# Attention scores of all eight heads at once, and one written order for the whole first feed-forward layer

## The chip, the core and the metric

The kernel runs on one core of a Trainium2 chip. The time is the device time of one execution in microseconds (us). The kernel before takes 810.61 us (median of 3 runs, 810.53 to 813.6). Its engines are TensorE (PE; its weight loads stand apart as PEld), VectorE (DVE), ScalarE (ACT), GpSimd (POOL) and SyncE (SP), whose queue issues all the kernel's DMAs.

## The reference

Nyström attention over 4 batches, 8 heads, 576 tokens and head size 64, with 32 landmarks (means of 18 tokens each), is followed by two feed-forward layers over the 2304 tokens (512 to 2048 to 512). Inputs come as 64-bit floats.

```python
q_lm = q.reshape(B, H, 32, S // 32, D).mean(axis=3)      # k_lm likewise
A, Bm, C = sm(q, k_lm), sm(q_lm, k_lm), sm(q_lm, k)      # sm: softmax(a @ b.T / 8)
for _ in range(6):
    Z = 2 * Z - Z @ Bm @ Z                               # towards the inverse of Bm
attn = A @ Z @ C @ v
x = attn.transpose(0, 2, 1, 3).reshape(B * S, H * D)
h = x @ w_in;  g = h * clip(h + 3, 0, 6) / 6;  x = g @ w_out      # first layer
h = x @ w_in2; g = where(h > 0, h, exp(min(h, 0)) - 1); out = g @ w_out2
```

## The kernel before

**Slots.** The attention's last product is folded into the first layer's weights, so that the first layer is 128 slots: 4 batches by 2 halves of the tokens by 16 blocks of 128 hidden columns. A half has 288 tokens (320 and 256 in batch 0). In a slot, `slot_a1` makes 6 matmuls of the hidden block (tile h), ACT and DVE apply the activation (gf), ACT and POOL split the result into a rounded part and its rest (gh, gl), and three slots later (`DELAY`) `slot_a2` makes 12 matmuls (tile x): 4 column blocks by the three products of split operands. The 16 slots of batch 0's first half use unsplit operands (g, ub) instead: 4 full-precision matmuls, each of which the profile shows as two instructions. Slots 0 to 15 also convert the first layer's weights from 64 bits.

**Attention of the next batch.** Between the slots of one batch, the next batch's attention is computed ("newton" in the code): `prep` (landmark sums lm on DVE; POOL spreads them into a block-diagonal tile bd with zeros), `score_b` (Bm from lm and bd), `score_c` (C from kt and bd, giving EC), `soft` (A from qt and bd, giving ea), `values` (EC transposed through PE, times v), `inverse` (the iteration, tiles BD, BT and X), `finish`, and `attn_n` (folds the result into the weights w1c, giving nh and nl). Scores are made for one group g of 4 heads at a time: two pairs of heads in each, a matmul with 128 contracted rows and 64 output rows for each pair. All these products go through two PSUM buffers, tile bk; h has two and x four.

**Order.** Up to the end of batch 1 (`second_half`) the order on each engine is written out in PLAN1, one letter for a step ("s" a part of a slot, "c" a step of score_c). From `newton(2)` on, the tile framework's scheduler orders the instructions, by priorities that `wanted` sets and a few dependencies (`gated`, `after`). The second layer's weights are converted there too, one part in every second slot (`conv_out2`, `conv_in2`, `to_dram`): SP loads 64-bit words (tile u), ACT takes two steps, DVE two, POOL one, and the result y is stored when the next part has been loaded (`flush`).

**After slot 127** the second layer begins: `quartet`, `second`, `wino2`.

In the code `act`, `vec`, `pool` and `pe` are thin wrappers that, while `strict[0]` holds, chain each engine's instructions in the order of the code. As nearly every instruction is recorded by such a wrapper, the profile puts nearly all of them on line L116.

Of the kernel before, what the change touches and what calls it, by code (L numbers as in the profile page):

```python
# [31 lines left out]
def nystrom_ffn_kernel(ctx: ExitStack, tc, q, k, v, w_in1, w_out1, w_in2, w_out2, out):  # L32
# [43 lines left out]
    RUN = 6  # L76
# [27 lines left out]
    NAT = 25, 28, 31  # L104

# [265 lines left out]
    PLACES = [f"wo{(kk - 2) % (NKT + 1)}" for kk in range(NKT + 1)]  # L371
# [78 lines left out]
    def load_in2(q):  # L450
# [3 lines left out]
        for kk in range(2):  # L454
# [23 lines left out]
            gated(vec.tensor_tensor(out=f[:, 1], in0=f[:, 0], in1=l[:, 2], op=ALU.add))  # L478
            sub(f[:, 2], f[:, 1], l[:, 0])
            yield  # L480
            gated(sub(f[:, 3], l[:, 1], f[:, 2]))
            sub(f[:, 0], l[:, 0], f[:, 0])
            yield
            gated(act.copy(out=hr[:, 0:3], in_=l[:, 0:3]))
            sub(lr[:, 0:3], l[:, 0:3], h[:, 0:3], pool)
            yield
            gated(act.copy(out=hr[:, 3:7], in_=f))
# [7 lines left out]
    kt_t, qt_t, kbd_t, qbd_t, kl_t = {}, {}, {}, {}, {}  # L495

    def load_qk(b, g, what):
        t = ap_.tile([128, 2, S], F32, name=what + "t", tag=what + "t", bufs=2)
        gated(sp.dma_start(out=t, in_=(k if what == "k" else q)[b, g]))
        raw_t[b, g, what] = t  # L500
# [71 lines left out]
    def score_c(b, g, sc):  # L572
# [23 lines left out]
        if 0 < b < B - 1:  # L596
            load_qk(b + 1, g, "k")
        return EC

    def soft(b, g):  # L600
# [9 lines left out]
        if 0 < b < B - 1:  # L610
            load_qk(b + 1, g, "q")
# [17 lines left out]

    def values(b, g, EC, cvs, sc):  # L630
# [5 lines left out]
        for j in range(RUN):  # L636
            atr(ct[j // JB][0:PRUN, 128 * (j % JB):128 * (j % JB) + 128], EC[:, j:S:RUN], ident)
        yield 1.0
# [112 lines left out]
    def newton(b):  # L751

        EB, sb, sc, cvs = newton_tiles()
        s = [SB * (b - 1) + (NEW if b > 1 else NEW1)]
        kept = {}

        def go(gen, n=99):
            for _ in range(n):
                wanted(s[0])
                try:  # L760
                    s[0] += next(gen) * (PACE if b > 1 else PACE1)
                except StopIteration:
                    return

        def keep(key, gen):
            kept[key] = yield from gen

        go(prep(b, 0))
        go(score_b(b, 0, sb, EB))
        go(keep(0, score_c(b, 0, sc)))  # L770
        go(soft(b, 0))
        go(values(b, 0, kept[0], cvs, sc))
        go(prep(b, 1))
        go(score_b(b, 1, sb, EB))
        inv = keep("Q", inverse(EB, sb))
        sC = keep(1, score_c(b, 1, sc))
        sA = soft(b, 1)
        go(inv, 1)
        go(sC, 2)
        go(inv, 1)  # L780
        go(sC)
        go(inv, 2)
        go(sA, 3)
        go(inv, 2)
        v1 = values(b, 1, kept[1], cvs, sc)
        go(v1, 2)
        go(inv, 2)
        go(sA)
        go(v1)
        go(inv)  # L790
        go(finish(b, kept, cvs, sc))

    PLAN = """  # L800
        wwwwwwwwwmwwlll0123xmykkklmmllklylkwklwbcbkwcblklBcClCacBCwCBwwicivxwwCaiviVaiviaivivaAiyiVAwwxiVyiAwAiaAxiwixViVxAtffwtwyttn
# [123 lines left out]
    def slot_a1(i):  # L925
# [15 lines left out]
        if i < NKT:  # L941
# [13 lines left out]
    def slot_a2(i, mm=smm):  # L955
# [3 lines left out]
        for dm in range(NDM):  # L959
# [3 lines left out]
            if i < NKT:  # L963
                mm(acc[dm], wo[kk][:, sl], gh, kk == 0, kk == NKT - 1)
# [314 lines left out]
    def splits():  # L1279
        for kk in range(NKT):  # L1280
            split_out1(kk)
            yield
# [8 lines left out]
    def first_half(units, n0):  # L1291
# [12 lines left out]
        for i in range(-PRE, NKT):  # L1304
# [25 lines left out]
        for i in range(NKT, END):  # L1330
# [10 lines left out]
    PLAN1 = "sslssssusluulssppllpppssssspspbssosssbsssspssoccbscscpsPacaosvvasvavsosPvPaPasPssossssssssBsPosPssPsPsCCBBsosoCssCsisCsssisiAssAisAsioVssAssVsoiiViVsiiioVsAissisisAsiottifsfssssossnssstnffsTonossnssossnTssnssssnssssssssnTs"  # L1341

    def second_half(slots):

        EB, sb, sc, cvs = newton_tiles()
        kept = {}
# [3 lines left out]

        def parts():
            for c in range(NW):
                yield from attn_n(1, c, 256)

        make = {
            "u": lambda: attn_at(0, 1), "o": splits, "l": lambda: loads(1), "f": lambda: finish(1, kept, cvs, sc), "n": parts,
            "i": lambda: keep("Q", inverse(EB, sb)), "t": lambda: attn_at(1, 0), "T": lambda: attn_at(1, 1),
        }
        for g in range(G):
            for name, gen in (  # L1360
                ("p", lambda g=g: prep(1, g)), ("b", lambda g=g: score_b(1, g, sb, EB)),
                ("c", lambda g=g: keep(g, score_c(1, g, sc))), ("a", lambda g=g: soft(1, g)),
                ("v", lambda g=g: values(1, g, kept[g], cvs, sc)),
            ):
                make[name.upper() if g else name] = gen
        gens = {"s": slots}
        for c in PLAN1.replace(" ", ""):
# [4 lines left out]
        for c in "upbcavPBCAViftnTo":  # L1372
# [171 lines left out]
```

## Time and profile before

| what | value |
|---|---|
| time, median of 3 runs | 810.61 us |
| the profiled execution's own time | 810.39 us |
| its span in the trace | 808.6 us |
| busy share of the span: PE, PEld, DVE, ACT, POOL | 97%, 86%, 67%, 57%, 52% |
| first slot's first matmul, slot 16's, second layer's | at 31.2, 90.2 and 425.7 us |
| PE busy and idle from 90.2 to 425.7 us | 328.5 and 7.0 us |

A matmul's duration in the trace runs from its start to the modelled end of its output, and the next one starts long before that. What a stretch of matmuls costs is therefore read from one start to the next.

### The profile page before, as it was taken

How to read it: one execution, taken by the hardware profiler on the slowest of the kernel's cores; microseconds unless marked ns; L12 is line 12 of the kernel's file. 1: busy time of each engine (PE TensorE's matmuls, PEld its weight loads, DVE VectorE, ACT ScalarE, POOL GpSimd, SP SyncE). 2: the span in 40 equal slices, each digit the busy share in tenths (PEclk: the TensorE clock that was granted, in tenths of full speed). 3: DMA queues.
4: the chain of work that ended last, by engine and by line, in shares of the span. 5: the costliest groups of instructions: out<-in, count | busy, mean ns of one | idle time of the engine just before them, and what ended most of it. 6: DMA issues, size and time to landing. Idle time of an engine off the chain costs nothing.

```text
span 808.6 us, 16376 instructions
## 1 busy us (share of the span) xinstructions
PE 783.2 (97%) x5928; PEld 697.1 (86%) x5928; DVE 541.5 (67%) x1092; ACT 462.0 (57%) x1012; POOL 418.3 (52%) x423
## 2 busy tenths in 40 slices
PE   7799999999999999999999999999999999999998
PEld 6566778789887889889999999888898889999998
DVE  6899677479645764356465777666655655777795
ACT  3687454655556656565555566556544544555562
POOL 2576576467555566464621786769661560223311
PEclk9899999999999999999999999999999999999999
DMA  9977932686667545741542777689998666867663
GB/s 322 404 218 235 304 107 90 206 258 215 205 215 257 162 145 170 235 160 62 184 161 74 260 262 265 236 305 345 387 383 305 225 226 238 278 234 257 226 198 112
DMA packets 115601, 184.58 MB, mean 228 GB/s; under 512 B 8576, under 2 KB 71552, under 8 KB 115520
## 3 DMA queue, kind: packets, MB, share of 16 engines
q1 hardware_dynamic: 115520, 183.54, 66.7%
q8 instruction: 47, 0.77, 0.4%
q14 instruction: 34, 0.28, 0.1%
HBM read 130.02 MB, written 53.48 MB: 227 GB/s over the span
## 4 chain that ended last, share of the span: by engine, by line
PE 71%; DMA 11%; DVE 7%; ACT 3%; issue 3%; POOL 3%; SPq 1%; DVEq 0%; POOLq 0%; ACTq 0%
PE x L116 38%; PE h L116 30%; PE bk L116 4%; DMA u<-in_moe_w_out 3%; DMA qt<-in_q 2%; DVE h L116 1%; DMA kqv<-in_v 1%; DMA un<-in_moe_w_in 1%; DMA ub<-in_moe_w_out 1%; DMA w1d<-w1c 1%; SPq L116 1%; DVE w1c L116 1%; DMA w<-wo2d 1%; DVE lm L116 1%; DVE nl L116 1%
## 5 line engine op out<-in xcount | busy, mean ns | idle before, releaser
L116 PE MATMUL h<-x,wi 128*128 128x384 f32 x1008 | 204.7, 338 | 2.3 <-ACT a L116 1.5
L116 PE MATMUL x<-gh,wo 128*128 128x288 f32 (+1 forms) x896 | 199.3, 297 | 1.5 <-ACT xs L116 1.0
L116 PEld LDWEIGHTS h<-x,wi 128*128 128x128 f32 x1008 | 177.8, 188 | 13.1 <-ACT a L116 2.4
L116 PEld LDWEIGHTS x<-gh,wo 128*128 128x128 f32 x896 | 149.5, 188 | 9.9 <-issue 6.0
L116 PE MATMUL x<-gl,wo 128*128 128x288 f32 (+1 forms) x448 | 131.6, 294 | 0.3 <-DVE gl L116 0.3
L116 ACT CAST gh<-gf 128x288 fp32r<-128x288 f32 (+2 forms) x160 | 72.6, 454 | 88.2 <-DVE gf L116 87.9
L116 POOL TENSOR_TENSOR gl<-gf,gh 128x288 fp32r<-128x288 f32 (+1 forms) x100 | 83.0, 832 | 74.9 <-ACT gh L116 68.8
L116 PE MATMUL x<-w,gh 128*128 128x512 f32 (+1 forms) x360 | 101.8, 356 | 0.1
L116 DVE SCALAR_TENSOR_TENSOR gf<-gf,y 128x384 f32<-128x384 f32 x80 | 65.5, 819 | 33.1 <-ACT gf L116 33.1
L116 PE MATMUL h<-atl,nh 128*128 128x288 f32 (+2 forms) x256 | 81.8, 319 | 4.5 <-DVE nl L116 2.3
L116 PEld LDWEIGHTS x<-gl,wo 128*128 128x128 f32 x448 | 84.3, 188 | 1.6 <-issue 0.9
L116 ACT ACTIVATE gf<-h,half_b 128x288 f32<-128x288 f32 (+2 forms) x128 | 63.7, 498 | 37.3 <-PE h L116 32.0
L116 DVE SCALAR_TENSOR_TENSOR gf<-gf,h 128x288 f32<-128x288 f32 (+1 forms) x112 | 49.5, 443 | 43.7 <-ACT gf L116 42.7
L116 PE MATMUL x<-w,ghl 128*128 128x512 f32 (+1 forms) x324 | 76.7, 356 | 0.2 <-DVE ghl L116 0.2
L116 PE MATMUL h<-ath,nl 128*128 128x288 f32 (+2 forms) x256 | 76.7, 300 | 0.0
L116 ACT ACTIVATE gf<-y 128x384 f32<-128x384 f32 x80 | 42.0, 525 | 60.5 <-DVE y L116 60.4
L116 PE MATMUL h<-ath,nh 128*128 128x288 f32 (+2 forms) x256 | 76.4, 298 | 0.0
L116 PEld LDWEIGHTS x<-w,gh 128*128 128x128 f32 x360 | 64.7, 189 | 6.4 <-ACT gh L116 0.5
L116 PEld LDWEIGHTS h<-atl,nh 128*128 128x128 f32 x256 | 48.6, 190 | 18.5 <-issue 9.0
L116 PE MATMUL x<-w,gl 128*128 128x512 f32 (+1 forms) x180 | 64.2, 357 | 0.0
L116 POOL TENSOR_TENSOR x<-u,gf 128x384 f32<-128x384 f32 x16 | 18.1, 1151 | 85.2 <-DVE gf L116 50.9
L116 PEld LDWEIGHTS x<-w,ghl 128*128 128x128 f32 x324 | 55.2, 189 | 5.9 <-DVE ghl L116 0.4
(182 smaller groups left out, 1526.2 us busy)
## 6 DMA issues: line engine op xcount, KB each, us to landing
wi<-wi2p SPq DMA_DIRECT2D x64, 448.0 KB, 5.8
wi2p<-wi SPq DMA_DIRECT2D x32, 448.0 KB, 2.9
u<-in_moe_w_in SPq DMA_DIRECT2D x25, 512.0 KB, 4.8
w1c<-w1d SPq DMA_DIRECT2D x48, 256.0 KB, 4.3
w<-wo2p SPq DMA_DIRECT2D x24, 512.0 KB, 6.7
ub<-in_moe_w_out SPq DMA_DIRECT2D x16, 512.0 KB, 10.2
u<-in_moe_w_out SPq DMA_DIRECT2D x16, 512.0 KB, 5.3
wo2p<-w SPq DMA_DIRECT2D x16, 512.0 KB, 3.9
```

Source lines behind the costliest of these rows:

```text
L116: inst = getattr(self.eng, name)(*a, **kw)
```

## The change

Six things change.

1. Batches 1 to 3 make their scores for all 8 heads together (`prep8`, `score_b8`, `score_c8`, `soft8`). The helper `products` makes, for a half of the tokens, 8 matmuls with 64 contracted rows and 32 output rows: no block-diagonal tile, no zeros. The key landmarks stand in the key tile's first 32 columns, so that Bm comes out of the same matmuls as C's first half. For this the host hands over the odd group with the two heads of each pair in swapped rows for these batches, and the softmax of C is written back into the key tile. Each call of `products` takes both bk buffers. The part of C that shared a bank with Bm is copied out by ACT first.
2. The order is written out (PLAN1 anew, PLAN2, PLAN3, `ending`) for the whole first layer; `newton` and the scheduler's freedom there are gone.
3. The second layer's weights are converted by `conv_stream`, two parts loaded ahead; a converted part is stored ahead of the next load instead of behind it. Steps "z" of the plans place it.
4. Slots 14 and 15 use split operands (`FULL = 14`), so that their 8 full-precision instructions each become 12 split ones, and their weights are split in steps "h".
5. The start's plan (PLAN) has another order, with 30 warming matmuls instead of 25, and slots 1 and 2 have 3 and 4 instead of 7 and 2.
6. Some dependencies (`gated`) of the second layer's first weights go.

```diff
+    FULL = 14
-        if i < NKT:
+        if i < FULL:
             g = gp.tile([128, T2], F32, name="g", tag="gh")[:, 0:nt]
...
+    def products(ps, w, x, gs):
+        for pr in range(2):
+            for a in range(2):
+                o = 64 * pr + 32 * a
+                for i, g in reversed(list(enumerate(gs))):
+                    r = slice(64 * (a ^ g), 64 * (a ^ g) + 64)
+                    amm(ps[i][o:o + 32, :], w[i][r, pr, :], x[i][r, pr, :], True, True)
...
+    def score_c8(b, gs, sc, first):
+        kt, ql = [kt_t[b, g] for g in gs], [ql_t.pop((b, g)) for g in gs]
+        EC = [t[:, 0, 32:] for t in kt]
+        cut = 0, 32 + HALF, 32 + S
+        for hf in range(2):
+            ps.append([bank()[:, 0:cut[hf + 1] - cut[hf]] for _ in gs])
+            products(ps[hf], ql, [t[:, :, cut[hf]:cut[hf + 1]] for t in kt], gs)
+            yield 0.4
+            if hf == 0 and b:
+                for i in n:
+                    act.copy(out=EC[i][:, 0:HALF], in_=ps[0][i][:, 32:])
...
+    def soft8(b, gs):
+        for hf in range(2):
+            sa.append([bank()[:, 0:HALF] for _ in gs])
+            products(sa[hf], [t[:, :, 0:32] for t in kt], [t[:, :, hf * HALF:(hf + 1) * HALF] for t in qt], gs)
...
+    def conv_stream():
+        def begin():
+            o, src, k = conv.pop(0)
+            u = room()
+            y = stg.tile([128, W], F32, name="y", tag="y", bufs=YB)
+            gen = steps(src, u, y.rearrange("p (k n) -> p k n", k=k) if k > 1 else y)
+            next(gen)
+            return gen, o, y
+        nxt = [begin(), begin()]
+        while nxt[0]:
+            gen, o, y = nxt.pop(0)
+            flush()
+            nxt.append(begin())
+            yield
+            for _ in gen:
+                yield
+            pending.append((o, y))
...
-                for _ in range((2, 7, 2)[i]):
+                for _ in range((2, 3, 4)[i]):
...
-    second_half(first_half(units, n0))
-    strict[0] = False
-    newton(2)
+    batch(1, PLAN1, first_half(units, n0), zs, (256,))
+    for b, plan in ((2, PLAN2), (3, PLAN3)):
+        batch(b, plan, slots_of(SB * b - SB + 4, SB * b + 4), zs)
+    ending(slots_of(NA - SB + 4, NA), zs, load_x(0, vec), load_in2(0))
+    strict[0] = False
```

How this moves instructions is shown at three places. On PE, the first score products of batch 3 stood so before (lm with bd is Bm's product, kt with bd a half of C's for one group; h and x are slots):

```order
L116 MATMUL bk<-lm,bd 64x32 x2
L116 MATMUL x<-gh,wo_1966 128x288
L116 MATMUL x<-gl,wo_1966 128x288
L116 MATMUL bk<-kt,bd 64x288 x2
L116 MATMUL x<-gh,wo_1966 128x288 x2
L116 MATMUL x<-gl,wo_1966 128x288
L116 MATMUL x<-gh,wo_1966 128x288
```

Now the products of both groups, Bm's among them, stand in one block of 8 matmuls:

```order
L117 MATMUL x<-gh,wo_1451 128x288
L117 MATMUL bk<-kt,lm 32x320 x8
L117 MATMUL x<-gh,wo_1451 128x288
L117 MATMUL x<-gl,wo_1451 128x288
L117 MATMUL x<-gh,wo_1451 128x288 x2
```

Such a batch had 16 matmuls of 64 by 288 and 4 of 64 by 32; it now has 8 of 32 by 320 and 24 of 32 by 288, in four blocks. The second place is PE at the start of the inverse of batch 2 (BD and BT fill one bk buffer each, and DVE reads both). Before:

```order
L116 MATMUL bk<-BD,onesbd 128x128
L116 MATMUL x<-gh,wo_1873 128x288
L116 MATMUL x<-gl,wo_1873 128x288
L116 MATMUL bk<-BT 32x32 x8
L116 MATMUL x<-gh,wo_1873 128x288
L116 MATMUL h<-atl,nh_1884 128x288
L116 MATMUL h<-ath,nl_1885 128x288
L116 MATMUL h<-ath,nh_1884 128x288
```

Now:

```order
L117 MATMUL bk<-BD,onesbd 128x128
L117 MATMUL bk<-BT 32x32 x8
L117 MATMUL x<-gh,wo_1648 128x288
L117 MATMUL x<-gl,wo_1648 128x288
L117 MATMUL x<-gh,wo_1648 128x288
L117 MATMUL bk<-qt,kt 32x288 x8
```

Before, 34 slot matmuls stood between BT and the next bk product; now 3 do, and the product behind them wants both bk buffers. The third place is SP's queue where the second layer's weights begin to be converted (u is a load, wo2d the store of a converted part, w1c folded weights). Before:

```order
L116 DMA u<-in_moe_w_out 128x1024
L116 DMA w1c<-w1d 128x4x128 x4
L116 DMA wo2d<-y 128x512
L116 DMA u<-in_moe_w_out 128x1024
L116 DMA wo2d<-y 128x512
L116 DMA w_5896<-wo2d 128x512
```

Now:

```order
L117 DMA w1c<-w1d 128x4x128 x4
L117 DMA u<-in_moe_w_out 128x1024 x3
L117 DMA w1c<-w1d 128x4x128 x4
L117 DMA wo2d<-y 128x512
L117 DMA u<-in_moe_w_out 128x1024
L117 DMA w_5915<-wo2d 128x512
L117 DMA wo2d<-y 128x512
```

Three loads now stand ahead of the first store; behind it stores and loads alternate. PE's order in the second layer is the same as before.

## Rows read from the trace of the kernel before

**Rows 1.** Stretches: length, busy PE, PEld, DVE, ACT, POOL; clock, DMA share, GB/s.

```profile
0.00:31.20 31.20, 22.65 (x345) 17.01 (x345) 22.80 (x72) 12.58 (x32) 10.42 (x31) 0.98 0.96 351
31.20:90.20 59.00, 55.22 (x367) 39.57 (x367) 52.20 (x96) 45.62 (x93) 40.34 (x32) 0.95 0.82 266
90.20:425.70 335.50, 328.46 (x3096) 290.72 (x3096) 206.20 (x458) 194.44 (x456) 185.85 (x205) 1.00 0.56 181
425.70:808.60 382.90, 376.91 (x2125) 349.85 (x2124) 260.30 (x468) 209.37 (x433) 181.70 (x155) 1.00 0.73 254
```

**Rows 2.** Groups of PE instructions, 90.2 to 425.7 us: the three score products.

```profile
L116 PE MATMUL bk<-qt,bd 128*64 128x288 f32 x48 | 8.3, 429 | 0.6 <-ACT EC L116 0.4 <-DVE nn L116 0.2
L116 PE MATMUL bk<-kt,bd 128*64 128x288 f32 x48 | 8.0, 426 | 0.1
L116 PE MATMUL bk<-lm,bd 128*64 128x32 f32 x24 | 2.1, 233 | 0.7 <-POOL bd L116 0.7
```

**Rows 3.** PE in order of time (start, us, instruction) around score blocks of batch 3.

```profile
254.15 0.29 PE L116 MATMUL x<-gl,wo 128*128 128x288 f32 x1
254.38 0.71 PE L116 MATMUL bk<-kt,bd 128*64 128x288 f32 x4
255.01 0.53 PE L116 MATMUL x<-gh,wo 128*128 128x288 f32 x2
...
272.39 0.31 PE L116 MATMUL bk<-lm,bd 128*64 128x32 f32 x4
272.62 0.40 PE L116 MATMUL h<-atl,nh 128*128 128x288 f32 x1
...
277.58 1.19 PE L116 MATMUL bk<-kt,bd 128*64 128x288 f32 x8
278.70 0.40 PE L116 MATMUL h<-atl,nh 128*128 128x288 f32 x1
278.94 0.29 PE L116 MATMUL h<-ath,nl 128*128 128x288 f32 x1
279.07 0.29 PE L116 MATMUL h<-ath,nh 128*128 128x288 f32 x1
```

**Rows 4.** PE in order of time around two blocks of 64 by 32 matmuls (attn_n).

```profile
151.29 0.66 PE L116 MATMUL bk<-w1c,mt 64*32 64x256 f32 x16
151.89 0.40 PE L116 MATMUL h<-atl,nh 128*128 128x288 f32 x1
...
333.09 1.09 PE L116 MATMUL bk<-w1c,mt 64*32 64x512 f32 x16
334.11 0.40 PE L116 MATMUL h<-atl,nh 128*128 128x288 f32 x1
```

**Rows 5.** PE in order of time around slot 12's full-precision matmuls.

```profile
87.91 0.31 PE L116 MATMUL h<-ath,nh 128*128 128x320 f32 x1
88.06 2.32 PE L116 MATMUL x<-g,ub 128*128 128x320 f32 x8
90.17 0.36 PE L116 MATMUL h<-atl,nh 128*128 128x256 f32 x1
```

**Rows 6.** Two of PE's waits, 90.2 to 425.7 us: in total, times, longest.

```profile
PE bk L116 <- DVE nl L116: 2.4, 3, 1.2
PE bk L116 <- POOL bd L116: 0.7, 2, 0.4
```

**Rows 7.** PE: a block of 64 by 32 matmuls that found a bk buffer taken.

```profile
146.81 0.99 PE L116 MATMUL bk<-w1c,mt 64*32 64x256 f32 x16 [0.42 <-DVE nl L116]
```

**Rows 8.** PE's BD in batch 0, and DVE's steps that read BD's and BT's buffers.

```profile
14.75 0.46 PE L116 MATMUL bk<-BD,onesbd 128*128 128x128 f32 x2 [0.72 <-DVE BT L116]
...
15.25 0.29 DVE L116 TENSOR_REDUCE nn<-bk 128x4 f32<-128x128 f32 x1 [0.43 <-PE bk L116]
...
16.25 0.41 DVE L116 SCALAR_TENSOR_TENSOR X<-bk,cc,istack 128x32 f32<-128x32 f32 x2
```

**Rows 9.** ACT's exponentials over a half of C (durations min, median, max).

```profile
L116 ACT ACTIVATE EC<-bk,mx x16: 484/493/501, 12.7 to 282.3; 128x288 f32<-128x288 f32 x16
```

**Rows 10.** DMA issues on SP, KB each, median us to landing.

```profile
ub<-in_moe_w_out SPq DMA_DIRECT2D x16, 512.0 KB, 10.2
u<-in_moe_w_out SPq DMA_DIRECT2D x16, 512.0 KB, 5.3
```

More of the change, by code (lines that the diff above doesn't have):

```diff
@@ L595, in score_c @@
             )
-        if 0 < b < B - 1:
-            load_qk(b + 1, g, "k")
         return EC
@@ L628, in soft, with prep8 @@
         e_t[b, g] = ea
+    def prep8(b, g):
+        x = kt_t[b, g] = raw_t.pop((b, g, "k"))
+        y = qt_t[b, g] = raw_t.pop((b, g, "q"))
+        lm = ql_t[b, g] = ap_.tile([128, 2, 32], F32, name="lm", tag="lmk", bufs=2)
+        for o, i in ((x[:, :, 0:32], x[:, :, 32:]), (lm, y)):
+            for r in (slice(0, 1), slice(1, 2)):
+                gated(vec.tensor_reduce(
+                    out=o[:, r], in_=i[:, r].rearrange("p r (l c) -> p r l c", c=POOL), axis=AX, op=ALU.add
+                ))
+                yield 0.7
@@ L749, in newton_tiles @@
         return EB, sb, sc, cvs
[L751 to L791, printed above, removed]
     PLAN = """
-        wwwwwwwwwmwwlll0123xmykkklmmllklylkwklwbcbkwcblklBcClCacBCwCBwwicivxwwCaiviVaiviaivivaAiyiVAwwxiVyiAwAiaAxiwixViVxAtffwtwyttn
+        wwlwkwwwl0w1wlmk2lww3lymxwykmlkmlykwkbwkbwkccbwlwyBClCalyclcBlCwCBwiwcxwvwiawvCiviawiaViviivaAiyiVAwxyxiViAwAiaAiwxixiVxVwAtfxwftywttwn
     """
@@ L1277, in nystrom_ffn_kernel, with splits @@
     NA = B * SB
-    def splits():
-        for kk in range(NKT):
+    def splits(kks):
+        for kk in kks:
             split_out1(kk)
@@ L1329, in first_half, with slots_of @@
         run(ns)
-        for i in range(NKT, END):
+        yield from slots_of(NKT, END)
+    def slots_of(n0, n1):
+        for i in range(n0, n1):
             wanted(i)
@@ L1345, in second_half, with batch, preps @@
+    def batch(b, plan, slots, zs, narrow=()):
         EB, sb, sc, cvs = newton_tiles()
-        kept = {}
+        kept, first, gs = {}, [], range(G)
         def keep(key, gen):
             kept[key] = yield from gen
+        def preps():
+            for g in gs:
+                yield from prep8(b, g)
         def parts():
             for c in range(NW):
-                yield from attn_n(1, c, 256)
+                yield from attn_n(b, c, *narrow)
         make = {
-            "u": lambda: attn_at(0, 1), "o": splits, "l": lambda: loads(1), "f": lambda: finish(1, kept, cvs, sc), "n": parts,
-            "i": lambda: keep("Q", inverse(EB, sb)), "t": lambda: attn_at(1, 0), "T": lambda: attn_at(1, 1),
-        }
@@ L1359, in second_half @@
[L1359 to L1367, printed above, removed]
+            "p": preps, "c": lambda: keep("C", score_c8(b, gs, sc, first)), "b": lambda: score_b8(gs, first, sb, EB),
@@ L1368, in second_half @@
+            "i": lambda: keep("Q", inverse(EB, sb)), "a": lambda: soft8(b, gs),
+            "v": lambda: values(b, 0, kept["C"][0], cvs, sc), "V": lambda: values(b, 1, kept["C"][1], cvs, sc),
+            "f": lambda: finish(b, kept, cvs, sc), "n": parts, "t": lambda: attn_at(b, 0), "T": lambda: attn_at(b, 1),
+        }
+        gens = {"s": slots, "z": zs, "u": attn_at(0, 1), "o": splits(range(FULL)), "l": loads(1), "h": splits(range(FULL, NKT))}
+        for c in plan:
             if c not in gens:
@@ L1371, in second_half, with ending @@
         run(slots)
-        for c in "upbcavPBCAViftnTo":
+        for c in "pcbiavVftnT":
             run(gens[c] if c in gens else make[c]())
-        for e in (act, vec, pool):
-            e.flow = e.last
+        if b == 1:
+            run(gens["o"])
+    def ending(slots, zs, xs, ws):
+        for i in range(NA - SB + 4, NA):
+            for n in range(NDM + 1):
+                next(slots, None)
+                if i < NA - SB + XSET + 4:
+                    next(zs, None)
+                elif n == 2:
+                    next(xs, None)
+                if i >= NA - 22 and n == 4:
+                    next(ws, None)
+        run(slots)
+        run(zs)
+        run(xs)
+        run(ws)
     win, xp = [], []
```

169 lines of the change are left out of this document (108 added, 61 removed).

## The prediction

> **What bounds the kernel now.** I read the stretches first [rows 1]. In the second layer, from 425.7 us on, PE is idle 382.9 - 376.9 = 6.0 us in 382.9. In the stretch that the change rebuilds, slots 16 to 127 with the attention of batches 1 to 3 between them (90.2 to 425.7 us), it is idle 335.5 - 328.5 = 7.0 us, while DVE, ACT and POOL are busy 61%, 58% and 55% of it, at full clock. So PE bounds both, and a matmul taken out of the stretch shortens it, as long as no wait takes its place. The 31.2 us before the first slot are a chain of loads and small steps (PE busy 22.7), and the 59 us of slots 0 to 15 are shared by PE (55.2) and DVE (52.2).
>
> Next I read what the scores cost PE. The groups count 48 + 48 + 24 instructions in the stretch [rows 2], but their durations overlap, so the price is read in order of time, from start to start [rows 3]. The usual step between slot matmuls is 0.13 us (278.94 to 279.07). A block of 4 instructions of 288 columns takes 255.01 - 254.38 = 0.63, one of 8 takes 278.70 - 277.58 = 1.12, one of 4 with 32 columns 272.62 - 272.39 = 0.23. Ahead of a block the step is 0.23 instead of 0.13 (254.15 to 254.38), and behind it 0.24 (278.70 to 278.94): every block costs another 0.2 us at its two ends.
>
> **The change part by part.**
>
> *Scores.* Batches 1 to 3 have 6 blocks of the small kind, 16 of four and 4 of eight (16 x 4 + 4 x 8 = 96, the two groups of 48; 6 x 4 = 24). That is 6 x 0.23 + 16 x 0.63 + 4 x 1.12 = 15.9 us, with 26 x 0.2 = 5.2 for the ends 21.1 us. The new blocks have 16 instructions each, of 64 by 32. The trace has this form in attn_n [rows 4]: 16 instructions of 256 columns take 151.89 - 151.29 = 0.60, of 512 columns 334.11 - 333.09 = 1.02, so 0.00164 a column: 0.65 at 288 and 0.70 at 320 columns. These blocks too go through the column groups in the outer loop and through the two row halves, each with its own bank, in the inner one, just as `products` does. Three batches have 3 x 0.70 + 9 x 0.65 = 8.0 us, and 12 x 0.2 = 2.4 for the ends: 10.4. The difference is -10.7 us. With bd gone, PE's waits for it go too, -0.7 [rows 6]. From below: if blocks with both row halves ran no better than one half at a time, the 0.00164 a column would double and the 12 blocks would cost 12 x 0.48 = 5.8 more, leaving -5.6. I take -11.4, since the form is measured in this very kernel.
>
> *Slots 14 and 15.* 8 full-precision instructions take 90.17 - 88.06 = 2.11 us; 12 split ones at the 320-column step of 0.15 (87.91 to 88.06) take 1.8 [rows 5]. Two slots: -0.6. The weights' split comes earlier and the rounded copies and rests of two slots are new, about 1 us each on ACT and POOL beside PE; the price is 0 if they are ready in time and some 1 us if x of slot 14 waits for them.
>
> *Two banks at a time.* Here the change adds waits. A score block for both groups needs both bk buffers, and PE runs in order, so that a block that finds one taken stops the slots behind it. The trace shows this wait: such a block of attn_n waits 0.42 us with its instruction stream spread out [rows 7], and these waits come to 2.4 us [rows 6]. The nearest place in the new order is behind BD and BT. From BD's start to the end of DVE's last read of BT's buffer it is 16.25 + 0.41 - 14.75 = 1.9 us [rows 8]. BD and BT with the three slot matmuls that now follow take about 0.7 + 0.4 = 1.1, so qt,kt waits some 0.8 us, in batch 2 and again in batch 3; in batch 1 the first X is as near: together 2.4. In batch 1 the two key blocks stand 18 slot matmuls of 256 columns (2.2 us) apart, while emptying the first takes a maximum, an exponential and a copy for each group, some 3 us, and behind the second four exponentials of 0.5 with their sums [rows 9]: up to 1 each, 2.0. Against these 4.4, of the 7.0 us of idle time that PE has there now, 6.3 without bd's, I expect half to go, since their places are written anew: -3.2. Net +1.2, with -4 (all present waits gone and half the new ones) and +8 (the bank waits nearly twice as long, all present waits still there) as its ends.
>
> *The Trainium skill on this.* "TensorEngine Tiling (Array Packing)", Restrictions and Gotchas, PSUM Pressure, says that row tiling raises the pressure on PSUM, because row tiles that run together write different banks. The trace agrees, with the 0.42 us above. By that rule alone the bank waits would be the price of the faster products; here that is the 4.4 us already in the sum, and the second rival if they grow.
>
> *Written order, conversions.* The number of conversion steps is unchanged, 32 parts of five instructions. In PLAN2 95 "z" steps at five a part make 19 parts in the 101 us of 32 slots, 5.3 us a part, and the load stands two parts ahead, over 10 us before ACT wants it. The loads land in 5.3 us [rows 10], so they are hidden; ACT's 6 new copies of half a C (some 3 us) lie beside PE, as ACT is idle 42% of the stretch. The earlier store only frees y sooner. Price 0; if the lead fails, the third rival.
>
> *Start.* The order of the start has changed, and there are 5 more warming matmuls early and 4 - 2 = 2 fewer in slots 1 and 2 on balance. The loads of q, k, v are as before. No row shows the new order; its bounds are -2 and +2 us (PE is idle 31.2 - 22.7 = 8.5 us there, and a quarter of it either way is what a reordering of the small steps may move). I take 0. The second layer's PE order is the same, so I take 0 there, with 1 us either way for when its first operands are ready.
>
> Sum: -11.4 - 0.6 + 1.2 = -10.8 us against the profiled execution's own 810.4 us, of which 808.6 is its span: 799.6. That execution lies 0.2 below the median of the runs, so I say 799.8.
>
> **The rivals.**
> *Everything in the order gets better too.* The new plans may remove most of the 7.0 us of idle time in the stretch, and some of the step ends, with hardly a new wait, and the start gains its 2 us: -11.4 - 0.6 - 4 - 2 = -18, 792.4. For it: letters that were moved one by one can fit what each step waits for. Against it: the new bank waits, which no order with two bk buffers avoids altogether.
> *Bank waits take it back.* The four score blocks, BD, BT and the transposes all take bk buffers in turn. At +8 for them the sum is -11.4 - 0.6 + 8 = -4, 806.4. For it: the 0.42 us wait and the 3 slot matmuls behind BT. Against it: in batches 2 and 3 the key blocks have 33 to 48 slot matmuls (4.4 to 6.4 us) behind each for DVE and ACT, but for the pair in batch 3 with 24.
> *Row halves don't run together.* Then -5.6 takes the place of -10.7: 804.9. Against it stand the two rows of attn_n.
> *Slower: loads hold ACT.* With every engine in a written order, an ACT step whose load hasn't landed stops the next slots' activations, and with two h buffers PE stops two slots later. It decides from the point where a load takes longer than its lead of about 10 us; ub, the same size, took 10.2 in the first stretch [rows 10], at a DMA share of 0.82 to 0.96 [rows 1] against 0.56 here. At 0.7 us for each of 32 loads it is +22 - 10.8, 821.8. For it: nothing in the stretch now, with its 5.3 us.
>
> **How the numbers follow.** The forecast, from 796 to 803, has a chance of 0.58; the better order 0.16; the bank waits 0.14; the halves 0.04; slower 0.08. What a measurement of this kernel can tell from no change is about 0.5%, 4 us: faster means below 806.6. The forecast, the better order, the halves and about 0.05 of the bank waits lie there, 0.83; the rest of the bank waits and 0.01 of the slower case lie within 0.5%, 0.10; slower is 0.07. A range of 792 to 806 leaves out the slower case, some of the bank waits and the tail of the better order.
>
> **What would show it.** In the profile after: the blocks of kt with lm and of qt with kt should take 0.65 to 0.70 us from start to start (1.13 if the halves don't overlap). Slot 16 should begin within 2 us of 90.2 and the second layer's first matmul at about 415 instead of 425.7, with the rest as long as now, 382.9. PE's waits for DVE's X and nn at bk should be near 1 us each in place of bd's. If ACT's waits for u are long and h waits for gf, the slower rival holds. The prediction is wrong if the stretch from 90.2 us shortens by less than 5 or more than 16 us, or if the gain lies elsewhere.

## The result and the profile after

The changed kernel takes 805.26 us (median of 11 runs, 803.13 to 808.08); the kernel before, on the same chip, 812.92 us. The ratio is 0.9918, with a 95% interval of [0.9895, 0.9941]; two more sets gave 0.9908 and 0.9917. So it is faster, by about 6.6 us of 810.6, where 10.8 were forecast. 805.26 us lies inside the range of 792 to 806, but outside the forecast's own 796 to 803; by the ratio it is 804.0 on the scale of 810.6 us, which lies between the same bounds.

The page of the profiled run (804.58 us, span 802.5), busy time by engine and the granted clock in 40 slices:

```profile
PE 777.6 (97%) x6014; PEld 697.7 (87%) x6014; DVE 537.7 (67%) x1092; ACT 465.2 (58%) x1020; POOL 411.7 (51%) x401
PEclk9799999999999999999999999999999999999999
```

Its stretches, as [rows 1] shows those of before (slot 16 begins at 89.9 us, the second layer at 417.75):

```profile
31.00:89.90 58.90, 55.18 (x360) 39.31 (x360) 52.21 (x96) 45.03 (x93) 41.25 (x33) 0.91 0.85 274
89.90:253.00 163.10, 159.49 (x1746) 139.19 (x1745) 101.23 (x245) 102.68 (x246) 96.96 (x99) 1.00 0.67 210
253.00:275.00 22.00, 18.06 (x143) 16.52 (x142) 19.00 (x46) 11.99 (x29) 12.90 (x12) 0.92 0.84 248
275.00:417.75 142.75, 142.17 (x1293) 133.58 (x1291) 79.89 (x170) 82.42 (x188) 69.10 (x71) 1.00 0.43 144
417.75:802.50 384.75, 377.54 (x2126) 349.73 (x2124) 261.81 (x469) 209.01 (x433) 181.03 (x155) 1.00 0.73 253
```

The rebuilt stretch has become 335.5 - 327.85 = 7.65 us shorter, where the sum had 10.8, and the second layer 1.8 longer. In the stretch nearly half of PE's idle time, 3.9 of 8.1 us, lies in 22 us around 260, where the granted clock is also low. The views of PE's waits from 89.9 to 417.7 us, to set beside [rows 6]:

```profile
PE h L117 <- DVE gf L117: 4.3, 2, 3.9
PE bk L117 <- ACT kt L117: 1.3, 2, 0.8
PE bk L117 <- DVE lm L117: 1.2, 1, 1.2
PE bk L117 <- DMA vt<-in_v: 0.6, 1, 0.6
PE bk L117 <- DVE nn L117: 0.4, 1, 0.4
```

Of before's waits only the one for nn is left, and a new one, for gf, is the longest. The score blocks themselves, in PE's order of time (start, duration, instructions, wait):

```profile
109.12 0.71 PE L117 MATMUL bk<-qt,kt 64*32 64x288 f32 x16
109.77 0.39 PE L117 MATMUL x<-gh,wo 128*128 128x256 f32 x1
...
176.23 0.49 PE L117 MATMUL bk<-BD,onesbd 128*128 128x128 f32 x2
177.22 0.33 PE L117 MATMUL bk<-BT 32*32 32x32 f32 x16 [0.51 <-ACT kt L117]
...
178.07 1.23 PE L117 MATMUL bk<-qt,kt 64*32 64x288 f32 x16
179.24 0.41 PE L117 MATMUL x<-gh,wo 128*128 128x288 f32 x1
...
277.60 1.53 PE L117 MATMUL bk<-qt,kt 64*32 64x288 f32 x16
279.06 0.40 PE L117 MATMUL x<-gh,wo 128*128 128x288 f32 x1
```

From start to start a free block takes 109.77 - 109.12 = 0.65 us, as forecast. Behind BD and BT of batch 2 it takes 1.17, the extra 0.52 inside the block; BT had already waited 0.51 for the other buffer. In batch 3 the same block takes 279.06 - 277.60 = 1.46, 0.81 more than a free one. The profile counts most of such a wait inside a block as PE's busy time, so the list above leaves it out. Of the twelve blocks six take 0.64 to 0.71 us, one 0.79 and five 0.95 to 2.66: 12.1 us in all with the waits inside them, where the sum had 8.0 without any.

The stop at 256 us, first PE, then ACT, DVE, GpSimd and SyncE in the same view:

```profile
255.57 0.29 PE L117 MATMUL x<-gh,wo 128*128 128x288 f32 x1
259.80 0.40 PE L117 MATMUL h<-atl,nh 128*128 128x288 f32 x1 [3.94 <-DVE gf L117]
...
261.18 0.44 PE L117 MATMUL x<-gh,wo 128*128 128x288 f32 x1
261.42 0.44 PE L117 MATMUL x<-gl,wo 128*128 128x288 f32 x1
...
253.10 0.43 ACT L117 CAST ath<-at 128x288 fp32r<-128x288 f32 x1
258.20 0.66 ACT L117 ACTIVATE y<-u 128x512 f32<-128x512 f32 x1 [4.67 <-POOL y L117]
258.77 0.48 ACT L117 ACTIVATE gf<-h,half_b 128x288 f32<-128x288 f32 x1
...
255.54 1.17 DVE L117 SCALAR_TENSOR_TENSOR y<-u,y 128x512 uint32<-128x512 uint32 x1
256.64 1.40 DVE L117 TENSOR_REDUCE kt<-kt 128x32 f32<-128x576 f32 x2
257.96 1.40 DVE L117 TENSOR_REDUCE lm<-qt 128x32 f32<-128x576 f32 x2
259.29 0.46 DVE L117 SCALAR_TENSOR_TENSOR gf<-gf,h 128x288 f32<-128x288 f32 x1
...
253.91 1.32 POOL L117 TENSOR_TENSOR y<-y,u 128x512 uint32<-128x512 uint32 x1 [1.68 <-issue]
...
255.25 0.33 SPq L117 DMA_DIRECT2D wi2d<-y  x1
```

This is the seam of two written plans. PLAN2 ends in `TzznzzzzzTz` and PLAN3 begins `ppzps`: nine conversion steps (z) and three landmark steps (p) stand between two slot steps (s); T and n are other attention steps. ACT can't begin the next part (y<-u, 258.20) before one of the two y buffers is free: GpSimd's sum of the part two before ends at 255.23, its store is issued at 255.25, and the stores here land in 2.1 to 2.9 us, up to 258.15. (The view names the next sum, which ends at 258.13, so this profile alone doesn't tell the two apart. In the two other profiles of the changed kernel it names the store, with 5.1 and 4.7 us.) The slot's gf on ACT stands behind that, at 258.77. On DVE two conversion steps and four landmark sums (2.8 us; the fourth is recorded two slot steps behind the seam) stand ahead of its gf, which comes at 259.29. Both queues would have held PE. ACT's wait in the second profile:

```profile
ACT y L117 <- DMA wi2d<-y: 5.1, 1, 5.1
```

Behind the stop the steps are 0.24 us (261.18 to 261.42) and not 0.13, in 16 matmuls, 16 x 0.11 = 1.8 us. In the stretches there the clock is the third figure from the end, and PE is idle 3.8 of 4 us ahead of its fall:

```profile
256.00:260.00 4.00, 0.20 (x1) 0.20 (x2) 4.00 (x7) 1.80 (x4) 1.44 (x2) 1.00 1.02 323
260.00:263.50 3.50, 3.50 (x16) 3.50 (x16) 2.57 (x6) 1.44 (x4) 1.65 (x2) 0.52 1.01 294
263.50:267.00 3.50, 3.50 (x37) 2.82 (x36) 2.63 (x9) 2.82 (x7) 2.41 (x3) 1.00 0.59 149
```

0.52 is the level of 1.2 GHz for nearly all of the 3.5 us. Stop and clock together cost 3.9 + 1.8 = 5.7 us.

The wait for lm comes from a load of u. ACT, DVE and PE where the conversions begin, in batch 2:

```profile
162.33 0.66 ACT L117 ACTIVATE y<-u 128x512 f32<-128x512 f32 x1 [2.56 <-DMA u<-in_moe_w_out]
...
163.02 0.43 DVE L117 TENSOR_SCALAR y<-y 128x512 uint32<-128x512 uint32 x1 [1.79 <-ACT y L117]
...
164.68 0.75 DVE L117 TENSOR_REDUCE lm<-qt 128x32 f32<-128x576 f32 x1
...
165.48 0.74 PE L117 MATMUL bk<-kt,lm 64*32 64x320 f32 x8 [1.25 <-DVE lm L117]
```

The first load of u is issued at 156.02, behind four loads of w1c. ACT waits for it from 159.77, DVE's conversion step waits for ACT, and the last landmark sum stands behind that step in DVE's order. In the three profiles of the changed kernel ACT waits 2.56, 3.06 and 1.95 us for this load, and PE 1.25, 1.75 and 0.66 us for lm, 1.3 less each time.

### The profile page after: what moved, and what is told of

It reads as the page before. It is cut to its first block, busy times and chain, and to the rows that moved or that the text cites. A ratio compares the mean times of both kernels' runs of the same rounds, so it can differ in the third digit from the quotient of the medians.

```text
span 802.5 us, 16527 instructions
## 1 busy us (share of the span) xinstructions
PE 777.6 (97%) x6014; PEld 697.7 (87%) x6014; DVE 537.7 (67%) x1092; ACT 465.2 (58%) x1020; POOL 411.7 (51%) x401
## 4 chain that ended last, share of the span: by engine, by line
PE 61%; DVE 3%; DMA 2%; POOL 1%; ACT 1%; issue 1%; DVEq 0%; ACTq 0%; POOLq 0%
PE x L117 33%; PE h L117 27%; PE bk L117 2%; DMA wi<-wi2d 1%; POOL x L117 1%; DMA x<-wo2d 1%; DVE u L117 0%; DVE y L117 0%; DVE gf L117 0%; DVE ghl L117 0%; DVE gl L117 0%; ACT gf L117 0%; ACT ghl L117 0%; DVE kt L117 0%; DVE lm L117 0%
## 5 line engine op out<-in xcount | busy, mean ns | idle before, releaser
L117 PE MATMUL x<-gh,wo 128*128 128x288 f32 (+2 forms) x912 | 207.2, 299 | 0.0
L117 PEld LDWEIGHTS x<-gh,wo 128*128 128x128 f32 x912 | 154.4, 189 | 14.0 <-issue 12.3
L117 PE MATMUL x<-gl,wo 128*128 128x288 f32 (+2 forms) x456 | 133.8, 293 | 0.0
L117 POOL TENSOR_TENSOR gl<-gf,gh 128x288 fp32r<-128x288 f32 (+2 forms) x102 | 84.8, 831 | 88.4 <-ACT gh L117 75.9
L117 ACT CAST gh<-gf 128x288 fp32r<-128x288 f32 (+3 forms) x162 | 73.7, 455 | 93.9 <-DVE gf L117 92.8
L117 DVE SCALAR_TENSOR_TENSOR gf<-gf,h 128x288 f32<-128x288 f32 (+2 forms) x114 | 50.6, 444 | 68.7 <-ACT gf L117 68.4
L117 DVE SCALAR_TENSOR_TENSOR gf<-gf,y 128x384 f32<-128x384 f32 x80 | 67.9, 849 | 34.3 <-ACT gf L117 34.2
L117 PEld LDWEIGHTS x<-gl,wo 128*128 128x128 f32 x456 | 86.3, 189 | 0.0
L117 POOL TENSOR_TENSOR x<-u,gf 128x384 f32<-128x384 f32 x16 | 18.1, 1151 | 85.1 <-DVE gf L117 50.9
## 6 DMA issues: line engine op xcount, KB each, us to landing
ub<-in_moe_w_out SPq DMA_DIRECT2D x16, 512.0 KB, 10.2
```

The lines of the kernel that those rows point to most:

```text
L117: inst = getattr(self.eng, name)(*a, **kw)
```

## The experiments

The table reads every profile by slots: a slot begins at the first of its 6 matmuls of h, so the starts are counted off PE's timeline. Times in us.

| kernel | slots 16-36 | 36-64 | 64-76 | 76-96 | second layer | ratio to before, 95% |
|---|---|---|---|---|---|---|
| before | 70.2 | 89.1 | 37.1 | 61.2 | 383.0 | 1 |
| after | 64.6 | 85.6 | 40.2 | 59.3 | 384.8 | 0.9918 [0.9895, 0.9941] |
| after, again | 65.2 | 87.5 | 40.6 | 59.3 | 383.6 | 0.9908 [0.9882, 0.9935] |
| after, third | 65.3 | 85.1 | 40.2 | 59.3 | 383.3 | 0.9917 [0.9893, 0.9941] |
| landmarks spread | 64.6 | 85.0 | 40.5 | 59.3 | 384.4 | 0.9903 [0.9873, 0.9933] |
| conversions spread | 67.2 | 86.9 | 39.6 | 59.3 | 383.0 | 0.9912 [0.9883, 0.9941] |
| both | 65.3 | 85.1 | 38.9 | 59.3 | 383.2 | 0.9884 [0.9854, 0.9915] |
| both, again | 65.5 | 84.3 | 39.2 | 59.3 | 383.9 | 0.9902 [0.9864, 0.9939] |
| both, w1c earlier | 65.1 | 87.4 | 38.1 | 59.3 | 384.0 | 0.9886 [0.9859, 0.9913] |
| thin seam | 64.9 | 86.6 | 36.0 | 69.1 | 382.7 | 0.9988 [0.9966, 1.001] |
| thin seam, steps put back | 65.2 | 87.2 | 40.8 | 68.5 | 383.2 | 1.0011 [0.9987, 1.0035] |
| thin seam, stores by GpSimd | 67.1 | 95.3 | 36.1 | 78.0 | 384.0 | 1.0172 [1.0141, 1.0203] |
| thin seam, w1c earlier | 67.1 | 87.1 | 36.0 | 63.5 | 384.2 | 0.9932 [0.9904, 0.9959] |
| store behind load | 66.0 | 90.3 | 42.7 | 61.1 | 382.6 | 1.001 [0.9989, 1.0032] |
| halves one by one | 65.7 | 85.7 | 40.2 | 59.3 | 383.3 | 0.9901 [0.987, 0.9933] |
| slots 14, 15 unsplit | 68.4 | 85.9 | 41.0 | 59.3 | 383.3 | 0.9913 [0.9886, 0.9939] |
| after, conversions late | 65.4 | 82.9 | 35.8 | 59.3 | not read | none |
| before, conversions late | 71.3 | 86.7 | 36.3 | 59.7 | not read | none |

How far one profile can be trusted shows in slots 16 to 36, whose order is the same in all kernels but the two of before and the one with slots 14 and 15 unsplit (with the halves one by one it differs inside the score blocks alone). They take 64.6 to 66.0 us in twelve profiles and 67.1 or 67.2 in three, in which the granted clock from 89 to 157 us was 0.97 instead of 1.00. Slots 36 to 64 differ by 2.4 us between the three profiles of the changed kernel.

**The seam.** The changed kernel again, and the two moves apart and together (each pair of lines is an excerpt of a plan; the blanks in it are there for reading alone):

> The changed kernel once more, on the same chip as the next three. Both theories: the stop of PE at 255.6 us (3.9 us, ended by DVE's gf) and the half clock behind it (0.76 granted between 260 and 267 us) stand at the same place, since every engine's order is fixed; the time is about 0.992 of before. The second layer's extra 1.8 us hangs on when one load lands (wi from wi2d, 5.6 us against 3.9 before): if that is chance, it is not the same in this profile; if the order causes it, it is.

```diff
 landmarks spread (PLAN3's start)
-ppzpsspzszzss sppssss sssss szzpspzcbcsszzs
+zspszpszzspsp sspspss spsspss szzszcbcsszzs
```

> Only the eight landmark steps at the start of batch 3's plan are spread, one or two between slot steps, instead of four in a row ahead of slot 68's second half; the conversions stay. Theory A (the written order holds PE at the seam of the two plans: on DVE four landmark sums, 2.8 us, on ACT a conversion that waits for its y buffer, stand ahead of gf): ACT's own gf still comes at 258.8, so at most 0.5 us is gained here, some -0.2 +- 1 us against the changed kernel. Theory B (DVE's queue alone sets the stop): 2 to 2.8 us less, and less of the half clock: -3 to -4 us.

```diff
 conversions spread (PLAN2's end, PLAN3's start)
-ssszss sssszzs ssszszs zszssss TzznzzzzzTz
+szsszss szssszzs ssszszs zszsszss TznzT
-sppssss sssss
+sppsszss szsszss
```

> Only six of the eight conversion steps at the end of batch 2's plan are moved, three to the slots ahead and three to the slots behind; the landmark steps stay in a row. Theory A: ACT's gf is free early, DVE loses three or four conversion steps of 0.4 to 1.2 us ahead of the landmark sums; the stop shrinks from 3.9 to 1 or 2 us: -2 to -3 us against the changed kernel. Theory B (DVE's queue alone): the same DVE steps go, -2 to -2.5. Theory C (the conversions' rate is what is short, so that moved steps wait elsewhere): within 1 us of the changed kernel, with new waits of PE for gf at other slots.

> Both moves. Theory A: the stop at the seam goes with the half clock behind it, 3.9 + 1.7 = 5.6 us less than the changed kernel, some -5 with a small wait left; about 799 to 800 us beside 810.4 for before, ratio 0.986. Theory B: as theory A, but most of it already in the run with the landmark steps alone. Theory C: -1 us at best, and the missing microseconds come up as waits for gf, lm or kt elsewhere in batches 2 and 3.

The stop stood at the same place again, 4.4 us long. The landmarks alone gained nothing in slots 64 to 76, as theory A had it and B not; the conversions alone some 0.8 us, less than expected, and nothing in the ratio. Both together brought 1.2 to 1.4 us there, each against the mean of the changed kernel's three profiles, and 2.4 to 3.0 in the sum of slots 36 to 96, not 5. PE's rows in that kernel show why:

```profile
256.50 0.40 PE L117 MATMUL h<-atl,nh 128*128 128x288 f32 x1 [1.14 <-DVE gf L117]
...
262.12 0.74 PE L117 MATMUL bk<-kt,lm 64*32 64x320 f32 x8 [0.79 <-DVE lm L117]
...
267.12 0.98 PE L117 MATMUL bk<-kt,lm 64*32 64x288 f32 x16 [0.89 <-ACT EB L117]
```

The long stop is now three short ones and one of 0.26 us, with the full clock (1.00) behind each, and the steps of DVE and ACT are as many as before. The pair of both moves and the changed kernel was run once more:

> The kernel with both moves once more, beside the changed kernel on one chip. Theory A (the stop and its half clock cost the changed kernel 5.6 us, of which a smaller wait for gf, lm and EB takes 3 back): 2 to 3 us less than the changed kernel. Rival (chance): within 1 us of it.

> The changed kernel beside the other three on one chip: ratio 0.991 to 0.992, the stop at the seam at the same place in the trace.

0.9902 against 0.9917, 804.5 against 805.3 us: the same sign, inside the intervals. A gain of 1 to 2 us is likely and not shown.

**Thinner still.** Eight conversion steps out of PLAN2's end and ten out of PLAN3's start (the last 32 of PLAN3 find nothing left to convert, so nothing is lost), batch 3's landmark steps spread, and batch 2's a few steps earlier (those aren't in the excerpt):

```diff
-zszssss TzznzzzzzTz  ppzpsspzszzss sppssss sssss szzpspzcbcsszzs
+zszssss TnT          spsspsps      spsspsps spspsss sscbcsss
```

> Around the seam of the plans of batches 2 and 3 the conversion steps are taken out (9 in batch 2's plan, 10 in batch 3's; the last 32 conversion steps of batch 3's plan did nothing so far, and now do), the landmark steps of batch 3 are spread, those of batch 2 moved a few steps ahead. Theory A (too many steps of other engines between two slot steps at the seam): no wait for gf, lm or EB is left between 250 and 270 us, no half clock there, and the wait for lm at 164 us shrinks: 5 to 7 us less than the changed kernel, 799 to 800 us beside 812 for before, ratio 0.984 +- 0.002. Theory C (the conversions' rate is short): the conversions that are now later collide with batch 3's scores, new waits for gf between 270 and 330 us, ratio 0.988 or more, no better than with both moves.

The seam did as expected: 36.0 us for slots 64 to 76, 4.2 to 4.6 less. The time did not: 6 to 7 us worse than the changed kernel. SyncE's queue and then PE, in order of time:

```profile
319.77 0.33 SPq L117 DMA_DIRECT2D u<-in_moe_w_in  x1
329.06 0.32 SPq L117 DMA_DIRECT2D wi2d<-y  x1
329.48 0.37 SPq L117 DMA_DIRECT2D u<-in_moe_w_in  x1
329.94 2.05 SPq L117 DMA_DIRECT2D w1c<-w1d  x4
...
337.09 1.96 PE L117 MATMUL bk<-w1c,mt 64*32 64x512 f32 x16 [7.06 <-DMA w1c<-w1d]
```

The store at 329.06 waits 9 us in the queue for GpSimd's sum, and the load of w1c stands behind it. Three kernels test this: the steps put back away from w1c, the stores issued by GpSimd, and w1c's load recorded one step earlier.

> As the kernel with the conversion steps taken out around the seam, but these steps are put back where they don't reach the loads of w1c: three more in the last slots of batch 2's plan, seventeen spread over slots 73 to 85, so that the conversions end at about the same slot as in the changed kernel. Theory D (two things decide: nothing but slot steps and landmark sums at the seam, and no store that waits for its data ahead of a w1c load in SP's queue): slots 64 to 76 stay at 36 us instead of 40.2, the wait of 7.1 us for w1c is gone, slots 76 to 96 at 59 to 61 us; 799 to 801 us, ratio 0.985 to 0.987. Theory C (the conversions' rate is short between slots 68 and 96): what the seam gains, slots 76 to 85 lose in waits for gf, ratio 0.991 or more.

> The kernel with the conversion steps taken out around the seam, and nothing else changed but that GpSimd's queue issues the stores of converted parts instead of SyncE's. Theory D (in that kernel PE's 7.1 us for w1c came of a store that waited for its sum in SP's queue, 319.8 to 329.1 us, with the load of w1c behind it): the w1c loads go out when PE frees their buffer, the wait is 0 to 1 us, the half clock behind it is gone, -7 to -9 us against that kernel, ratio 0.988 to 0.990, if issuing costs GpSimd little; each issue of a us there would lengthen gl and bring waits for gl instead. Rival (the load itself is late or slow, whatever stands ahead of it in the queue): the wait for w1c stays at 5 us or more, ratio 0.997.

```diff
 w1c earlier (attn_n, batches 2 and 3)
+            if b > 1 and o + n == W and nb < B:
+                load_w1(nb, nc_)
             yield
-        nb, nc_ = ...
-        if 0 < nb < B:
+        if b <= 1 and 0 < nb < B:
             load_w1(nb, nc_)
```

> The kernel with the conversion steps taken out around the seam, and the loads of w1c for batches 2 and 3 recorded one step of attn_n earlier, so that in SP's queue they stand ahead of up to three stores of converted parts; PE's order is the same. Theory D (the queue's order made the 7.1 us): no wait for w1c and no half clock behind it, slots 76 to 96 at 59 to 60 us instead of 69.1, slots 36 to 96 at 181 to 183; 798 to 801 us, ratio 0.984 to 0.987. Theory C (the number of conversions is the price): the wait moves to gf or to y, slots 36 to 96 stay at 187 us or more, ratio 0.991 or more.

> The kernel with both moves at the seam, with the same earlier loads of w1c. In it PE never waits for w1c, so theory D expects the time of the kernel with both moves within 1.5 us (ratio 0.986 to 0.990); if its remaining 1.3 us wait for gf at 255 us came of SP's queue (a store 1.8 us late behind eight w1c loads), up to 2 us less.

With w1c's load earlier, and PE's order the same, the wait for w1c is gone and slots 76 to 96 take 63.5 instead of 69.1 us: the queue's order had made it. The rest moved to gf (2.7 us at 343.5, and 0.79 granted behind it), so 0.9932 is still no better than the changed kernel. Theory D is half right. Putting the steps back between slots 73 and 85 took the seam's gain away (40.8 us again, with waits for bank buffers that ACT held) and PE stopped for 4.1 us for gf at 325 us, as theory C had it. With the stores on GpSimd's queue the wait for w1c stayed, 8.2 us: in SyncE's queue the loads of u, which wait for the same sum to free their buffer, now held it (three loads issued from 333.1 to 347.5, w1c's at 347.6). Here the Trainium skill has a rule: "DMA: Bandwidth & Descriptors", Issuing engines are not separate DMA queues, says that transfers of all issuers run on the same 16 engines and that another issuer saves only its time to issue. Nothing in the run speaks against it: from GpSimd's queue the stores landed in 4.6 us, no sooner than from SyncE's (2.3 and 3.1 in the changed kernel). On which engines they ran, and why they took longer, it doesn't show. That kernel lost another 8.7 us in slots 36 to 64 (95.3 against 86.6); each store took GpSimd some 0.9 us, but that this is the cause isn't shown.

**The order of store and load,** put back as it was before:

```diff
-            flush()
             nxt.append(begin())
+            flush()
```

> Only the converted part's store goes behind the next load again, as before the change. Theory A (the return of the y buffer stands on the chain that ends ACT's wait at the seam: add, store, landing, next step): each store comes later by the load ahead of it, 0.4 us of issue and what the load waits for, its u buffer; the stop at 255.6 us grows by 0.5 to 3 us, and ACT waits for y at other slots too: +1 to +4 us against the changed kernel. Rival (the forecast's price of 0, the store only has to come some time): the same time within 1 us.

It costs some 8 us: 7.5 to 8.3 by the ratios, 8.3 in slots 36 to 96 (194.0 against 185.7 in the mean). ACT's waits from 156 to 346 us in that kernel, and its stores' time to landing:

```profile
ACT y L117 <- DMA wi2d<-y: 15.0, 10, 3.8
ACT y L117 <- DMA wo2d<-y: 10.3, 7, 2.2
```
```profile
wo2d<-y SPq DMA_DIRECT2D x16, 256.0 KB, 4.5
wi2d<-y SPq DMA_DIRECT2D x16, 256.0 KB, 4.5
```

Behind a load of 512 KB a store lands in 4.5 us instead of 2.3 and 3.1, and ACT waits 25 us for y, where the changed kernel has 7.1 (4.7 at the seam and 2.4 for stores elsewhere). It was more than expected, and it came by theory A's way; how much of it is the later issue and how much the slower landing, the run doesn't part.

**Halves one by one,** and slots 14 and 15 unsplit (`FULL = 16`, their two "o" steps at slots 30 and 31):

```diff
-        for pr in range(2):
-            for a in range(2):
-                o = 64 * pr + 32 * a
-                for i, g in reversed(list(enumerate(gs))):
+        for i, g in reversed(list(enumerate(gs))):
+            for pr in range(2):
+                for a in range(2):
+                    o = 64 * pr + 32 * a
```

> Only the order of the eight score products of a block is changed: all four of one row half, then all four of the other. Theory A (the two row halves of the array run together only if they alternate): a block of 16 rows takes 1.13 us instead of 0.65 (1.25 for the 320 columns), 12 blocks, +5.8 us against the changed kernel where nothing else hides it, ratio about 0.998. Rival (the products overlap in any order, or a block's time goes by its columns of one half alone): 0.65 us and no change, 0.991.

```profile
109.85 0.72 PE L117 MATMUL bk<-qt,kt 64*32 64x288 f32 x16
110.49 0.38 PE L117 MATMUL x<-gh,wo 128*128 128x256 f32 x1
```

A block takes 0.64 us this way too: theory A is wrong, and the order of the halves is worth nothing.

> Slots 14 and 15 full-precision again, as before the change, their weights split in the steps behind. Theory A (the forecast's term): their x blocks take 2.1 instead of 1.8 us, +0.6 us against the changed kernel, too little for the interval of the ratio, so it is to be read in the trace: slot 17 to 19 longer by 0.3 each. Rival: the split's extra copies on ACT and POOL had cost as much: no difference from slot 14's start to slot 20's.

Slots 16 to 36 are 3 us longer, but 1.0 us of it is a new wait for nl, probably because the late weight splits fall among batch 1's steps (a wait of 0.7 for gf there is in two of the changed kernel's profiles too). The 0.6 could not be had apart.

**Without conversions.** All "z" letters taken out, the parts converted in one go ahead of the last slots; the same for the kernel before, whose 32 parts all came behind slot 96, from 351 us on:

```diff
 changed kernel: PLAN2, PLAN3 without z
+    run(zs)
     ending(...)
 kernel before
-        if (i - END) % O2 == 0 and conv:
+        while i == NA - SB + 3 and conv:
```

> The changed kernel with no conversion step in the plans of batches 2 and 3; the second layer's 32 parts are converted in one go ahead of the last slots, where PE then waits, so that only slots 36 to 96 are to be read (185.1 us with the conversions, 59.2 of them slots 76 to 96). Theory E (the forecast's price of 0 for the conversions in the written order is the term that failed): without them the stretch has no stop of more than 1.5 us, no half clock, and takes 176 to 179 us, 6 to 9 less. Rival (the score blocks' waits for two banks are what is missing): they stay, with 4 us or more of waits for kt, lm, nn and X at bk, and the stretch takes 182 us or more.

> The kernel before with 29 or more of its 32 conversions put behind slot 99; slots 36 to 96 are to be read (187.5 us with the conversions, 89.1 of them slots 36 to 64). Theory E': the scheduler's order hid the conversions, one part in two slots: the stretch stays within 2 us of 187.5; so conversions cost nothing before and 6 to 9 us now, and the gain of the scores alone is 187 - 177 = 10 us for batches 2 and 3 together. Rival (the conversions cost the same before): it falls by 5 us or more too, and the difference of the kernels without conversions is about as small as with them, 2 to 4 us.

Slots 36 to 64, 64 to 76 and 76 to 96 of the changed kernel without conversions, and the sum of the same slots of the kernel before without them:

```profile
154.60:237.50 82.90, 82.47 (x862) 74.00 (x855) 37.46 (x100) 37.10 (x92) 29.46 (x35) 1.00 0.39 119
237.50:273.40 35.90, 35.06 (x317) 30.56 (x315) 18.24 (x51) 16.99 (x47) 12.09 (x15) 1.00 0.27 76
273.40:332.70 59.30, 59.27 (x633) 53.47 (x630) 23.30 (x54) 25.50 (x59) 21.46 (x25) 1.00 0.20 57
```
```profile
sum 182.70, PE 182.70 PEld 160.18 DVE 76.47 ACT 80.28 POOL 66.77; mean PE 60.90 PEld 53.39 DVE 25.49 ACT 26.76 POOL 22.26
```

The three stretches of the changed kernel come to 178.1 us. So its conversions cost 185.1, 187.4 and 184.5 less 178.1: 7.0, 9.3 and 6.4 us, 7.6 in the mean. In the kernel before they cost 187.5 - 182.7 = 4.8, not 0 to 2: there my expectation was wrong and the rival nearer. Without them PE waits 1.3 us in the new order, 0.9 of it for X, and not at all in the old one; with them 6.4 and 2.9. (Waits inside blocks come on top: the blocks behind BD and BT take 1.74 and 1.76 us in the new order without conversions.) Stretch by stretch the conversions cost 3.2, 4.5 and 0 us now, in the mean, and 2.4, 0.8 and 1.5 before: what they cost more lies at the seam. The kernel before and the two without conversions stand in one profile each, so the totals are good to 1 or 2 us.

## Why the prediction was right and wrong

**The failed step is "Written order, conversions": "Price 0".** It looked at the load's lead, and that held for every load of u but the first, which had under 4 us instead of over 10 and stopped PE for 0.7 to 1.8 us by way of lm. ("Nothing in the stretch now" was misread, too: in the kernel before ACT waited 25.3 us for u in slots 36 to 96, in 13 waits, but PE didn't stop behind them.) It had said of the earlier store that it "only frees y sooner". But y has two buffers, and its way back, DVE's two steps, the sum, the store and its landing, is a chain that a written order can't give way to. Where nine conversion and three landmark steps meet between two slot steps it stops ACT, and PE with it. Measured, the conversions cost 7.6 us now and 4.8 before, 2.8 more, instead of 0 more. The 2.8 is good to some 2 us; the seam's part is sure: slots 64 to 76 take 40.2 to 40.6 us in the three profiles of the changed kernel, 36.0 with the thin seam and 35.8 without conversions. The average that I used, 5.3 us a part, says nothing of a place with nine steps in a row.

**PE as the bound, and the scores:** right. With conversions out of both kernels, slots 16 to 36 gain 71.3 - 65.4 = 5.9 us (4.9 to 5.6 in the profiles with conversions, which begin behind these slots), slots 36 to 96 4.6, and with the conversions where they belong slots 96 to 128 lose 0.3 (77.8 before, 78.1 after): 10.2 together, against 10.8 in the forecast's sum. Its parts are not all so good: by batch it came to 3.6, and batch 1 gave 5.9, batches 2 and 3 only 2.3 each. PE's idle time in the stretch came near the sum by luck: it grew by 1.1 us, from 7.0 to 8.1, where the terms give 4.4 - 3.2 - 0.7 = 0.5. What fell short is the busy time, 328.46 - 319.72 = 8.7 us less where 10.7 + 0.6 = 11.3 were forecast; 1.8 of the missing 2.6 is the half clock behind the stop, and waits inside blocks count as busy as well.

**Two banks at a time:** the waits are where they were put: about 1 us at BD, BT and the first block behind them in batch 2, 0.8 inside that block in batch 3, 0.8 at a key block of batch 1. The waits for X that were to be seen aren't there, and nn's is 0.4 and not 1. Most of the new idle time wasn't the banks': 3.9 of 6.4 us in slots 36 to 96 were for gf and 1.2 for lm, and old waits went nearly altogether, not by half. The Trainium skill's rule on PSUM pressure, cited there, is not contradicted (BT's 0.51), but it was not what the time hung on.

**Start and slots 14, 15:** in the three profiles slot 0 begins 0.6 to 1.1 and slot 16 0.2 to 0.8 us earlier, forecast 0; the 0.6 of the slots stays open.

**Second layer:** 1.8, 0.6 and 0.3 us longer in three profiles of the changed kernel, forecast 0 with 1 either way. The order there is the same. In the first PE waits 0.8 us at 497 us behind a load of wi that landed 5.5 us after its issue (3.8 before); in the other two that load took 5.0 and 5.3, and PE has no such wait. The rest stays open.

**The rivals.** "Bank waits take it back" named 806.4, near the time, for a wrong reason. "Loads hold ACT" had the kind of mechanism, a step of ACT that waits for a transfer and PE behind it, but the wrong transfer and 22 us instead of 2.8. "Row halves don't run together" is out as a price; whether they do overlap the runs don't say, since the order made no difference. (Its 804.9 should read 805.6: the -5.6 has bd's 0.7 in it already and takes the place of -11.4, not of -10.7.) "Better order" is out as a whole: the old waits went, as it had it, but new ones took their place.

Sum: 10.2 less 2.8 for the conversions and 0.3 to 1.8 in the second layer leaves 5.6 to 7.1 us, beside 6.6 by the ratio. With terms that are good to 1 or 2 us, so close a fit is partly luck.

## What to carry to other kernels

Price a written order by its densest place, not by its average: count, between two steps of the bounding engine, what stands on every other engine, and follow each buffer all the way back to free, through its sum, its store and the landing. An issue queue that is worked off in order is part of that count: a store or load that waits for its data holds every load behind it. To see what background work really costs, take it out of both kernels, and read the same stretch.

## What the runs showed that I had not expected

- A store of 256 KB issued just behind a load of 512 KB lands in 4.5 us, ahead of it in 2.3 (wi2d) and 3.1 (wo2d); in this kernel the one swap is worth some 8 us.
- A block of 16 instructions of 64 by 32 takes 0.65 us whether the two row halves alternate or come one after the other (0.64).
- Behind a stop of 3.9 us PE ran at half its clock for some 3.5 us; behind three stops of 1.1, 0.8 and 0.9 us in the same place the clock stayed at 1.00. Behind a stop of 1.8 us that ends at about 166 us it fell in one profile of the changed kernel (0.88 granted from 160 to 170 us) and not in that with the halves one by one (1.00): the length of the stop alone didn't settle it.
- The first load of u made ACT wait 2 to 3 us, and PE 0.7 to 1.8 us for another tile, lm, by way of DVE's order.
